# Attention scores as 64x64 matmuls in TensorE's four quadrants, plain buffers for the FFN's operands, and outputs nine f tiles behind the scores

## The chip, the cores and the metric

The kernel runs on one core of one Trainium2 chip. The metric is the device time of one execution in microseconds (us), and the time of a kernel is the median over its runs. Smaller is better.

## What is computed

There are 4 batches, 8 heads, 768 positions and a head dimension of 64. A banded attention feeds a two-layer FFN:

```python
k_sum = k.reshape(B, H, nb, block, D).max(axis=3)     # 24 blocks of 32 positions
v_sum = v.reshape(B, H, nb, block, D).mean(axis=3)
scores_l = scale * q @ k.T        # kept where |i - j| < 16, masked elsewhere
scores_s = scale * q @ k_sum.T + log(32)
a = softmax over [scores_l, scores_s]
x = a @ [v, v_sum]                # 3072 tokens of 512
h = max(x @ w_in, 0)              # w_in 512 x 2048
out = h * h @ w_out               # w_out 2048 x 512
```

## The kernel before, in words

**Tiles.** The 3072 positions are 24 tiles of 128, numbered g. Two tiles of x make a chunk c of 256 tokens, so there are 12 chunks. The FFN's hidden width is 16 f tiles of 128. One f tile of one chunk is called a slot. All operands are 32-bit. The FFN multiplies in a one-pass form with each operand split in a high and a low part (`xh`, `xl`, `gh`, `gl`, and two halves of `w_sb`). The attention multiplies plain 32-bit floats, and every such matmul in the code is two instructions in the trace.

**A slot.** `ffn1` (L318) issues 12 matmuls of 256 columns from `xh` and `xl` into a bank `ph`. `follow` then issues the 6 matmuls of 512 columns of `ffn2` (L359) for the slot two earlier (`BEHIND = 2`), with `gh` and `gl` as the stationary operand. Meanwhile ScalarE and VectorE take relu and square of `ph` (L327, L334, L339, L343).

**Attention of one tile, spread over the slots.** `steps` gives the pieces of tile g to ten steps, one step to a slot. Step 0 is `scores` (L222), steps 1 to 3 are mask, maximum and exponentials (`softmax`, L234 on VectorE, L242 on ScalarE), steps 3 and 4 the normalisation (L257), steps 5 to 7 the transposes (L270), step 8 is `outputs` (L283), step 9 is `split_x` (L301, L304), which makes `xh` and `xl`. What stands in `side` is issued in the middle of a slot, what stands in `last` at its end. A new tile begins every eight slots, so step 8 of tile g and step 0 of tile g+1 fall in the same slot, outputs first. The main loop handles tiles 6 to 23 and chunks 2 to 11.

**Scores before.** A tile's 128 queries are two groups s of 64, each with a window of 96 keys and 24 block sums, so 120 columns (`NK`). The contraction is 64 deep. `q_sb` is kept block-diagonal: partitions 0 to 63 hold group 0 in columns 0 to 63, partitions 64 to 127 hold group 1 in columns 64 to 127, and the rest is zero, set once by `memset` on GpSimd (L103). One 128x128 matmul per head then gives both groups, 8 per tile, into two buffers `s_ps` of four heads each. Loading q takes two DMAs per tile (L112). `place_k` (L157) copies the block maxima into `k_sb` with four VectorE copies.

**Outputs.** `outputs` issues 16 matmuls per tile with 64 stationary columns. Even heads write PSUM partitions 0 to 63, odd heads 64 to 127, so they use the two column halves of the array in turn.

**The start.** Tiles 0 to 5, the scores of tile 6, the preparation of the weights and the first 32 slots are issued in an order written out by hand, the string `START`: `S4.1` is `scores(4, 1)`, `TT` and `E` are the softmax of one head, `F1` and `F2` are `ffn1` and `ffn2`.

**The extra 32 bytes.** `shifted` makes the buffers of `xh`, `xl`, `gh` and `gl` 8 floats longer than needed (`SHIFT = 8`). The two or three buffers of each so begin at different addresses modulo 128 bytes: 64 and 96 for `xh`, 0 and 32 for `xl`, 64, 96 and 0 for `gh`, 32, 64 and 96 for `gl`. The weights `w_sb` all begin at 0 modulo 128.

Of the kernel before, what the change touches and what calls it, by code (L numbers as in the profile page):

```python
# [11 lines left out]
F32 = mybir.dt.float32  # L12
F32R = mybir.dt.float32r
# [16 lines left out]
NF = DF // P  # L30
NC4 = DM // P
SPARE = 1
SHIFT = 8
BEHIND = 2
NK = 96 + NB
MASKED = -1.0e9
# [20 lines left out]
F2.13 RE15v L:w13 SQ14 MU14 SQ15 MU15 F1.16 LO12a GL14v GL15v NR4.1 TT4.1 N4.1p S5.1 RE16a TT4.2 E4.1 TT4.3 MU16  # L57
F1.17 SQ16 TT4.0 E4.3 GL16v E4.2 SH12 S5.0 E4.0 RE17v AD12 F1.18 MU17 L:k7 NR4.0 L:v5 L:w15 F2.14 RE18a N4.0v
L:w14 HI13 MU18 F1.19 LO13v SQ17 CA12a GL17v SH13 F2.15 RE19a SU12v F1.20 SQ18 AD13 EV1.1v EV1.0a MU19 F2.16
GL18v RE20v CA11v F1.21 SQ19 MU20 GL19v HI15 SU11v F2.17 RE21a LO15v CA13a F1.22 MU21 SH15 SQ20 F2.18 RE22a  # L60
SU13p GL20v HI14 MU22 F1.23 SQ21 LO14a GL21v AD15 F2.19 RE23v MU23 F1.24 SQ22 SH14 CA15a GL22v AD14 F2.20 RE24v
MU24 T4.0 SQ23 F2.21 SU15p TT5.2 GL23v E5.2 TT5.1 TT5.3 T4.1 E5.1 TT5.0 F2.22 SQ24 TT5.4 TT5.5 TC4.1a GL24v
CA14a TT5.6 S6.0 TT5.7 TC4.0v E5.5 F2.23 SU14v E5.6 E5.7 S6.1 E5.0 E5.4 F1.25 E5.3 NR5.1 N5.1v F2.24 RE25v NR5.0
SQ25 MU25 F1.26 N5.0v GL25v T5.1 RE26a F1.27 SQ26 TC5.1v MU26 GL26v F2.25 RE27a SQ27 MU27 GL27v F1.28 F2.26
RE28v MU28 SQ28 GL28v F1.29 EV2.1v EV2.0v O4 RE29a SQ29 MU29 GL29v F1.30 XH4a XL4v F2.27 RE30a MU30 F1.31 SQ30
GL30v F2.28 RE31v MU31 T5.0 SQ31 F2.29 TC5.0v GL31v O5 XH5a L:v7 L:q7 XL5v L:v6
"""


# [1 line left out]
def attn_ffn_kernel(ctx: ExitStack, tc: tile.TileContext, q, k, kt, v, vt, v0, w, masks, ident, mean, out):  # L71
# [27 lines left out]
    vsum = const.tile([P, NPAIR, 32], F32, name="vsum")  # L99

    nc.vector.memset(vsum, 0.0)
    for t_ in q_sb + [e_sb] + pT:
        nc.gpsimd.memset(t_, 0.0)  # L103

    def copy(eng, out, in_):
# [15 lines left out]
    def load_v(g):  # L121
        nc.sync.dma_start(out=v_sb[g % 2][0:96], in_=v[g // NT, g % NT])
# [28 lines left out]
        nc.vector.tensor_scalar_mul(vsum[:, p, 0:NB], vsum[:, p, 0:NB], 1.0 / BLOCK)  # L151

    def place_k(g):
        dst = k_sb[g % 2].rearrange("a k (p two) j -> a k p two j", two=2)
        for par in range(2):
            for s in range(2):
                nc.vector.tensor_copy(  # L157
                    out=dst[s * 64 : s * 64 + 64, 4, :, par, :], in_=ksum[par * 64 : par * 64 + 64]
                )
# [55 lines left out]
    xh, xl = {}, {}  # L215
    s_ps, nmx, sm = {}, {}, {}

    def scores(g, half):
        s_ps[half] = ps_s.tile([P, 4, P], F32, name="s_ps")
        for i in range(4):  # L220
            h = half * 4 + i
            nc.tensor.matmul(  # L222
                s_ps[half][:, i, 0:NK], lhsT=q_sb[g % 2][:, h, :], rhs=k_sb[g % 2][:, :, h, :], start=True, stop=True
            )

    def mask_max(g, h):

        t = g % NT
        m = mask_sb[:, 0 if t == 0 else 2 if t == NT - 1 else 1, :]
        half, i = divmod(h, 4)  # L230
        if half not in nmx:
            nmx[half] = work.tile([P, 4], F32, name="nmx", tag="nmx", bufs=3)
            sm[half] = work.tile([P, 4], F32, name="sm", tag="sm", bufs=3)
        nc.vector.tensor_tensor_reduce(  # L234
            out=e_sb[:, h, 0:NK], in0=s_ps[half][:, i, 0:NK], in1=m, scale=-scale, scalar=3.0e38,
            op0=ALU.add, op1=ALU.min, accum_out=nmx[half][:, i : i + 1],
        )

# [48 lines left out]
                    start=True, stop=True,  # L287
                )

    def shifted(n, name, bufs):  # L290

        return work.tile([P, n + SHIFT], F32R, name=name, tag=name, bufs=bufs)[:, 0:n]

    def x_part(x, name, g):
        c, o = divmod(g, TPC)
        if c not in x:
            x[c] = shifted(NPAIR * CT, name, 2).rearrange("p (a b) -> p a b", b=CT)
        return x[c][:, :, o * P : (o + 1) * P]

    def high_x(g):  # L300
# [29 lines left out]
        return r  # L330

    def high_square(r):
        gh = shifted(CT, "gh", 3)
        nc.scalar.activation(gh, r, AF.Square)  # L334
        return gh

# [2 lines left out]
        nc.vector.tensor_mul(out=ph, in0=ph, in1=r)  # L339

    def low_square(ph, gh):
        gl = shifted(CT, "gl", 3)
        nc.vector.tensor_sub(out=gl, in0=ph, in1=gh.bitcast(F32))  # L343
        return gl

# [57 lines left out]
    def steps(g):  # L403


        b, t = divmod(g, NT)
        side, last = [[] for _ in range(10)], [[] for _ in range(10)]
# [3 lines left out]
        last[0] += [lambda: scores(g, 0), lambda: scores(g, 1)]  # L411
        if g + 2 < n_g:
            last[0].append(lambda: load_qk(g + 2))
        side[1].append(lambda: softmax(g, 0, 2))
        side[2].append(lambda: softmax(g, 2, 5))
        side[3] += [lambda: inverse(0), lambda: norm(0, nc.gpsimd), lambda: softmax(g, 5, 8)]
        side[4] += [lambda: inverse(1), lambda: norm(1, nc.gpsimd)]
        for n in range(3):
            side[5 + n].append(lambda n=n: turn(g, 4 * n, 4 * n + 4))
        last[8].append(lambda: outputs(g))  # L420
        if g + 2 < n_g:
            last[8].append(lambda: load_v(g + 2))
# [38 lines left out]
    def begin(op, i, j, eng):  # L461
# [14 lines left out]
            sum_v(1, i)  # L476

        elif op == "S":
            scores(i, j)
        elif op == "TT":  # L480
            mask_max(i, j)
        elif op == "E":
# [37 lines left out]
    with tc.manual_schedule(engines=None):  # L520
        for token in START.split():
            what, i, j, eng = re.fullmatch(r"(L:[a-z]+|F[12]|[A-Z]+)\.?(\d*)\.?(\d*)([avp]?)", token).groups()
            i, j = int(i or 0), int(j or 0)
            if what.startswith("L:"):
                load(what[2:], i)
            else:
                begin(what, i, j, engines.get(eng))
        tiles = {g: steps(g) for g in range(6, n_g)}

        def at(side, last, g, step):  # L530

# [85 lines left out]
```

## Time and profile before

| | |
|---|---|
| median of 3 runs | 664.42 us (664.35 to 664.96) |
| the profiled execution: its own time | 663.47 us |
| the profiled execution: span from first to last instruction | 661.7 us |
| mean granted TensorE clock | 0.992 |
| TensorE busy | 633.0 us, 4668 matmul instructions |
| VectorE, ScalarE, GpSimd busy | 404.9, 301.1, 110.6 us |
| bytes moved by DMA | 61.87 MB |

The profile is one execution, so its durations are held against its own 663.47 us, 0.95 us below the median. A row of the grouped lines reads: line, engine, operation, output<-inputs, shape, count | busy us, mean ns of one | idle time before, and what ended it. A row of the timeline reads: start, duration, engine, line, operation, and how many instructions in a row were merged. Matmuls are pipelined, and the ends of the recorded ones overlap the next ones' starts, so what a stretch of matmuls costs is read from starts alone.

### The profile page before, as it was taken

How to read it: one execution, taken by the hardware profiler on the slowest of the kernel's cores; microseconds unless marked ns; L12 is line 12 of the kernel's file. 1: busy time of each engine (PE TensorE's matmuls, PEld its weight loads, DVE VectorE, ACT ScalarE, POOL GpSimd, SP SyncE). 2: the span in 40 equal slices, each digit the busy share in tenths (PEclk: the TensorE clock that was granted, in tenths of full speed). 3: DMA queues.
4: the chain of work that ended last, by engine and by line, in shares of the span. 5: the costliest groups of instructions: out<-in, count | busy, mean ns of one | idle time of the engine just before them, and what ended most of it. 6: DMA issues, size and time to landing. Idle time of an engine off the chain costs nothing.

```text
span 661.7 us, 12338 instructions
## 1 busy us (share of the span) xinstructions
PE 633.0 (96%) x4668; PEld 566.5 (86%) x4668; DVE 404.9 (61%) x1247; ACT 301.1 (46%) x854; POOL 110.6 (17%) x87
## 2 busy tenths in 40 slices
PE   1788999999999999999999999999999999999997
PEld 1477999888889889999899998899898899988996
DVE  4678787656664684874863675865765645645332
ACT  2778867524424435335344344343444443443322
POOL 5464573401011011010010010010010110110000
PEclk9879999999999999999999999999999999999999
DMA  9999525005203314303103133212022020000000
GB/s 326 367 363 376 151 73 209 1 33 136 64 1 97 103 57 144 112 1 97 42 24 97 28 133 112 97 49 64 32 65 64 33 64 25 33 2 1 33 1 32
DMA packets 42314, 61.87 MB, mean 94 GB/s; under 512 B 27792, under 2 KB 27920, under 8 KB 40208
## 3 DMA queue, kind: packets, MB, share of 16 engines
q1 hardware_dynamic: 42256, 61.10, 28.3%
q8 instruction: 36, 0.59, 0.4%
q14 instruction: 22, 0.18, 0.1%
HBM read 54.80 MB, written 6.29 MB: 92 GB/s over the span
## 4 chain that ended last, share of the span: by engine, by line
PE 92%; DVE 3%; DMA 2%; ACT 1%; issue 1%; POOL 1%; SPq 0%; DVEq 0%; POOLq 0%; ACTq 0%
PE ph L318 41%; PE o_ps L359 39%; PE s_ps L222 7%; PE x_ps L283 3%; PE ph L263 1%; PE o_ps L129 1%; DMA kv<-in_kt 1%; DMA q_sb<-in_q 1%; DVE pT L270 1%; ACT e_sb L242 1%; DVE k_sb L157 0%; POOL e_sb L257 0%; DVE ksum L143 0%; POOL q_sb L103 0%; DVE ph L339 0%
## 5 line engine op out<-in xcount | busy, mean ns | idle before, releaser
L318 PE MATMUL ph<-xh,w_sb 128*128 128x256 f32 x1536 | 285.3, 284 | 0.7 <-ACT xh L301 0.7
L318 PEld LDWEIGHTS ph<-xh,w_sb 128*128 128x128 f32 x1536 | 248.3, 190 | 15.8 <-ACT xh L301 0.8
L359 PE MATMUL o_ps<-w_sb,gh 128*128 128x512 f32 x768 | 241.4, 395 | 0.0
L318 PE MATMUL ph<-xl,w_sb 128*128 128x256 f32 x768 | 217.0, 283 | 0.2 <-DVE xl L304 0.2
L339 DVE TENSOR_TENSOR ph<-ph,r 128x256 f32<-128x256 f32 x192 | 82.6, 431 | 157.1 <-ACT r L327 153.8
L327 ACT ACTIVATE r<-ph 128x256 f32<-128x256 f32 x179 | 68.2, 381 | 204.9 <-PE ph L318 203.7
L359 PE MATMUL o_ps<-w_sb,gl 128*128 128x512 f32 x384 | 151.3, 394 | 0.0
L318 PEld LDWEIGHTS ph<-xl,w_sb 128*128 128x128 f32 x768 | 145.5, 189 | 0.5 <-DVE xl L304 0.4
L359 PEld LDWEIGHTS o_ps<-w_sb,gh 128*128 128x128 f32 x768 | 131.1, 188 | 17.1
L257 POOL TENSOR_TENSOR e_sb<-e_sb,sm 128x480 f32<-128x480 f32 x42 | 41.7, 994 | 421.6 <-DVE nmx L234 360.9
L242 ACT ACTIVATE e_sb<-e_sb,nmx 128x120 f32<-128x120 f32 x192 | 73.9, 387 | 57.4 <-DVE nmx L234 57.4
L343 DVE TENSOR_TENSOR gl<-ph,gh 128x256 fp32r<-128x256 f32 x192 | 81.3, 424 | 29.7 <-ACT gh L334 7.1
L270 DVE STREAM_TRANSPOSE pT<-e_sb 32x256 f32<-32x256 f32 x216 | 94.2, 436 | 5.4 <-POOL e_sb L257 2.1
L334 ACT ACTIVATE gh<-r 128x256 fp32r<-128x256 f32 x192 | 80.4, 418 | 20.3 <-DVE r L329 7.7
L359 PEld LDWEIGHTS o_ps<-w_sb,gl 128*128 128x128 f32 x384 | 72.0, 188 | 17.1
L222 PE MATMUL s_ps<-k_sb,q_sb 128*128 128x120 f32 x384 | 51.4, 286 | 14.9 <-DVE k_sb L157 14.7
L222 PEld LDWEIGHTS s_ps<-k_sb,q_sb 128*128 128x128 f32 x384 | 46.9, 197 | 17.0 <-POOL w_sb L212 14.5
L234 DVE CUSTOM_DVE_ANT_0 e_sb<-s_ps,mask_sb 128x120 f32<-128x120 f32 x192 | 43.8, 274 | 5.3 <-PE ph L263 3.1
L205 POOL TENSOR_TENSOR w_raw<-w_raw 128x1024 int32<-128x1024 int32 x16 | 32.0, 2005 | 37.4 <-DVE w_raw L201 17.3
L242 ACT ACTIVATION_READ_ACCUMULATOR e_sb<-e_sb,nmx 128x1 f32 x192 | 36.1, 188 | 0.0
L283 PEld LDWEIGHTS x_ps<-pT,v_sb 128*64 128x64 f32 x768 | 24.4, 138 | 12.7 <-issue 9.5
L304 DVE TENSOR_TENSOR xl<-x_ps,xh 128x512 fp32r<-128x512 f32 x24 | 16.5, 688 | 27.0 <-ACT xh L301 27.0
(41 smaller groups left out, 293.0 us busy)
## 6 DMA issues: line engine op xcount, KB each, us to landing
w_raw<-in_w SPq DMA_DIRECT2D x16, 1024.0 KB, 10.7
k_sb<-in_k SPq DMA_DIRECT2D x24, 384.0 KB, 3.9
v_sb<-in_v SPq DMA_DIRECT2D x24, 384.0 KB, 3.7
kv<-in_kt SPq DMA_DIRECT2D x16, 384.0 KB, 5.3
q_sb<-in_q SPq DMA_DIRECT2D x48, 128.0 KB, 3.7
out<-ob SPq DMA_DIRECT2D x24, 256.0 KB, 2.0
kv<-in_vt SPq DMA_DIRECT2D x12, 384.0 KB, 4.9
vn<-in_v SPq DMA_DIRECT2D x2, 768.0 KB, 8.5
```

What stands on the lines that cost most here:

```text
L222: nc.tensor.matmul(s_ps[half][:, i, 0:NK], lhsT=q_sb[g % 2][:, h, :], rhs=k_sb[g % 2][:, :, h, :], start=True, stop=True)
L234: nc.vector.tensor_tensor_reduce(out=e_sb[:, h, 0:NK], in0=s_ps[half][:, i, 0:NK], in1=m, scale=-scale, scalar=3.0e38, op0=ALU.add, op1=AL ...
L242: nc.scalar.activation(e, e, AF.Exp, bias=nmx[half][:, i : i + 1], scale=-1.0, accum_out=sm[half][:, i : i + 1])
L257: eng.tensor_mul(out=e, in0=e, in1=sm[half].unsqueeze(2).to_broadcast([P, 4, NK]))
L270: nc.vector.transpose(out=pT[g % 2][j * 32 : j * 32 + 32, :, i * 32 : i * 32 + 32], in_=e_sb[i * 32 : i * 32 + 32, :, j * 32 : j * 32 + 32],)
L283: nc.tensor.matmul(xp[o : o + 64, h // 2, s * 64 : s * 64 + 64], lhsT=v_sb[g % 2][:, s, h * 64 : h * 64 + 64], rhs=pT[g % 2][:, h, s * 64 ...
L318: nc.tensor.matmul(ph, lhsT=w_sb[f][:, w, cc * P : (cc + 1) * P], rhs=x[c][:, cc, :], start=(n == 0), stop=(n == 3 * NC4 - 1))
L327: nc.scalar.activation(r, ph, AF.Relu)
L334: nc.scalar.activation(gh, r, AF.Square)
L339: nc.vector.tensor_mul(out=ph, in0=ph, in1=r)
L343: nc.vector.tensor_sub(out=gl, in0=ph, in1=gh.bitcast(F32))
L359: nc.tensor.matmul(o_ps[c][tt], lhsT=g_[:, ts_], rhs=w_sb[f][:, w, DM:], start=(first and n == 0), stop=(last and n == 2),)
```

## The change

Scores become 16 matmuls per tile with a contraction of 64 rows and 64 stationary columns: head parity r picks the row half of the array and the PSUM bank, query group s picks the column half. q is stored without zeros and comes in one DMA; k is stored by parity, and its block maxima are placed with one copy. One buffer `s_ps` of two banks takes the place of two of one bank. The FFN's operands lose the extra 32 bytes: each of their buffers now begins at 64 modulo 128, `w_sb` still at 0. The steps become eleven: outputs are step 9, `split_x` is step 10, and the loop starts every tile one slot earlier, so that outputs stay in their slot, scores and softmax come a slot before where they were, and scores and outputs no longer share a slot. In `START` the scores of tile 5 are both issued after the last mask of tile 4.

```diff
-SHIFT = 8
...
-F1.17 SQ16 TT4.0 E4.3 GL16v E4.2 SH12 S5.0 E4.0 RE17v AD12 F1.18 MU17 L:k7 NR4.0 L:v5 L:w15 F2.14 RE18a N4.0v
+F1.17 SQ16 TT4.0 S5.1 E4.3 GL16v E4.2 SH12 S5.0 E4.0 RE17v AD12 F1.18 MU17 L:k7 NR4.0 L:v5 L:w15 F2.14 RE18a
...
-    ps_s = ctx.enter_context(tc.tile_pool(name="ps_s", bufs=2, space=bass.MemoryType.PSUM))
+    ps_s = ctx.enter_context(tc.tile_pool(name="ps_s", bufs=1, space=bass.MemoryType.PSUM))
...
-    k_sb = [const.tile([P, 5, H, NB], F32, name=f"k_sb{i}") for i in range(2)]
+    k_sb = [const.tile([P, 5, 2, NPAIR, NB], F32, name=f"k_sb{i}") for i in range(2)]
-    q_sb = [const.tile([P, H, P], F32, name=f"q_sb{i}") for i in range(2)]
+    q_sb = [const.tile([P, 2, NPAIR, 64], F32, name=f"q_sb{i}") for i in range(2)]
...
-    for t_ in q_sb + [e_sb] + pT:
+    for t_ in [e_sb] + pT:
         nc.gpsimd.memset(t_, 0.0)
...
-        for s in range(2):
-            ps = slice(s * 64, s * 64 + 64)
-            nc.sync.dma_start(out=q_sb[g % 2][ps, :, ps], in_=q[g // NT, g % NT, ps])
+        nc.sync.dma_start(out=q_sb[g % 2], in_=q[g // NT, g % NT])
...
-        dst = k_sb[g % 2].rearrange("a k (p two) j -> a k p two j", two=2)
-        for par in range(2):
-            for s in range(2):
-                nc.vector.tensor_copy(
-                    out=dst[s * 64 : s * 64 + 64, 4, :, par, :], in_=ksum[par * 64 : par * 64 + 64]
-                )
+        nc.vector.tensor_copy(out=k_sb[g % 2][:, 4], in_=ksum.unsqueeze(1).to_broadcast([P, 2, NPAIR, NB]))
...
-    def scores(g, half):
-        s_ps[half] = ps_s.tile([P, 4, P], F32, name="s_ps")
-        for i in range(4):
-            h = half * 4 + i
-            nc.tensor.matmul(
-                s_ps[half][:, i, 0:NK], lhsT=q_sb[g % 2][:, h, :], rhs=k_sb[g % 2][:, :, h, :], start=True, stop=True
-            )
+    def scores(g, p0, p1):
+        if g not in s_ps:
+            s_ps[g] = ps_s.tile([P, 2, NPAIR, P], F32, name="s_ps")
+        for p in range(p0, p1):
+            for r, s in ((0, 0), (1, 1), (0, 1), (1, 0)):
+                rs, ss = slice(r * 64, r * 64 + 64), slice(s * 64, s * 64 + 64)
+                nc.tensor.matmul(
+                    s_ps[g][ss, r, p, 0:NK], lhsT=q_sb[g % 2][rs, s, p, :], rhs=k_sb[g % 2][rs, :, s, p, :],
+                    start=True, stop=True,
+                )
...
-            x[c] = shifted(NPAIR * CT, name, 2).rearrange("p (a b) -> p a b", b=CT)
+            x[c] = work.tile([P, NPAIR, CT], F32R, name=name, tag=name)
...
-        gh = shifted(CT, "gh", 3)
+        gh = work.tile([P, CT], F32R, name="gh", tag="gh", bufs=3)
...
-        gl = shifted(CT, "gl", 3)
+        gl = work.tile([P, CT], F32R, name="gl", tag="gl", bufs=3)
...
-        last[8].append(lambda: outputs(g))
+        last[9].append(lambda: outputs(g))
...
-        side[9].append(lambda: split_x(g))
+        side[10].append(lambda: split_x(g))
...
-        softmax(6, 0, 2)
+        softmax(6, 0, 5)
...
-                at(side, last, 2 * c + 2, f + 2)
-                at(side, last, 2 * c + 3, f - 6)
-                at(side, last, 2 * c + 4, f - 14)
+                at(side, last, 2 * c + 2, f + 3)
+                at(side, last, 2 * c + 3, f - 5)
+                at(side, last, 2 * c + 4, f - 13)
```

The order of TensorE's instructions in the main loop, around the outputs of an odd tile (`v_sb_82`) and the scores of the next, even one (`k_sb_79`), each row with its line, operation and tiles, and with how many in a row are alike. Before:

```order
L359 MATMUL o_ps<-w_sb,gh 128x512 x2
L359 MATMUL o_ps<-w_sb,gl 128x512
L283 MATMUL x_ps<-pT_87,v_sb_82 64x64 x16
L222 MATMUL s_ps<-k_sb_79,q_sb_83 128x120 x8
L318 MATMUL ph<-xh,w_sb 128x256 x2
L318 MATMUL ph<-xl,w_sb 128x256
```

After the change the scores stand alone at the end of a slot (the lines are those of the new code: L218 scores, L280 outputs, L311 `ffn1`, L352 `ffn2`):

```order
L352 MATMUL o_ps<-w_sb,gh 128x512 x2
L352 MATMUL o_ps<-w_sb,gl 128x512
L218 MATMUL s_ps<-k_sb_79,q_sb_83 64x120 x16
L311 MATMUL ph<-xh,w_sb 128x256 x2
L311 MATMUL ph<-xl,w_sb 128x256
```

One slot, that is 12 rows, further on stand the outputs of the tile before:

```order
L352 MATMUL o_ps<-w_sb,gh 128x512 x2
L352 MATMUL o_ps<-w_sb,gl 128x512
L280 MATMUL x_ps<-pT_87,v_sb_82 64x64 x16
L311 MATMUL ph<-xh,w_sb 128x256 x2
L311 MATMUL ph<-xl,w_sb 128x256
```

The scores, now 16 matmuls of 64 stationary columns, moved one slot ahead of the outputs, and both now have FFN matmuls on either side.

The second place is the beginning of VectorE's list, where the block maxima of batch 0 (`ksum`) are placed for tiles 0 and 1 and the masks of tile 0 follow. Before:

```order
L143 TENSOR_REDUCE ksum<-kv 128x24 x4
L157 COPY k_sb_79<-ksum 64x4x24 x4
L157 COPY k_sb_80<-ksum 64x4x24 x4
L234 ISA e_sb,nmx<-s_ps,mask_sb 128x120
L234 ISA nmx 128x1
```

After the change:

```order
L140 TENSOR_REDUCE ksum<-kv 128x24 x4
L151 COPY k_sb_79<-ksum 128x192
L151 COPY k_sb_80<-ksum 128x192
L231 ISA e_sb,nmx<-s_ps,mask_sb 128x120
L231 ISA nmx 128x1
```

Eight copies have become two, and nothing else moved in these rows.

More of the change, by code (lines that the diff above doesn't have):

```diff
@@ L234, in mask_max @@
         nc.vector.tensor_tensor_reduce(
-            out=e_sb[:, h, 0:NK], in0=s_ps[half][:, i, 0:NK], in1=m, scale=-scale, scalar=3.0e38,
+            out=e_sb[:, h, 0:NK], in0=s_ps[g][:, h % 2, h // 2, 0:NK], in1=m, scale=-scale, scalar=3.0e38,
             op0=ALU.add, op1=ALU.min, accum_out=nmx[half][:, i : i + 1],
@@ L288, in outputs @@
                 )
-    def shifted(n, name, bufs):
-        return work.tile([P, n + SHIFT], F32R, name=name, tag=name, bufs=bufs)[:, 0:n]
     def x_part(x, name, g):
@@ L406, in steps @@
         b, t = divmod(g, NT)
-        side, last = [[] for _ in range(10)], [[] for _ in range(10)]
+        side, last = [[] for _ in range(11)], [[] for _ in range(11)]
         if b and t < 2:
@@ L410, in steps @@
             side[6].append(lambda: place_v(g))
-        last[0] += [lambda: scores(g, 0), lambda: scores(g, 1)]
+        last[0].append(lambda: scores(g, 0, NPAIR))
         if g + 2 < n_g:
@@ L419, in steps @@
             side[5 + n].append(lambda n=n: turn(g, 4 * n, 4 * n + 4))
-        last[8].append(lambda: outputs(g))
+        last[9].append(lambda: outputs(g))
         if g + 2 < n_g:
-            last[8].append(lambda: load_v(g + 2))
-        side[9].append(lambda: split_x(g))
+            last[9].append(lambda: load_v(g + 2))
+        side[10].append(lambda: split_x(g))
         if b and t in (3, 4) and b + 1 < B:
@@ L478, in begin @@
         elif op == "S":
-            scores(i, j)
+            scores(i, 2 * j, 2 * j + 2)
         elif op == "TT":
@@ L530, in at @@
         def at(side, last, g, step):
-            if g in tiles and 0 <= step < 10:
+            if g in tiles and 0 <= step < 11:
                 side += tiles[g][0][step]
@@ L571, in _layouts @@
 def _layouts(q, k, v):
-    qt = q.reshape(B, H, NT, 2, 64, D)
-    qd = np.zeros((B, NT, 2, D, H, 64), q.dtype)
+    qd = q.reshape(B, NPAIR, 2, NT, 2, 64, D).transpose(0, 3, 2, 6, 4, 1, 5)
     kp = np.zeros((B, H, S + 2 * WINDOW, D), k.dtype)
```

27 lines of the change are left out of this document (13 added, 14 removed).

## The prediction

> **What bounds the kernel now.** I read the page first, then the busy time by stretches, the groups by shape, and TensorE's timeline around one tile. The page's busy line and its chain of work:
>
> ```profile
> PE 633.0 (96%) x4668; PEld 566.5 (86%) x4668; DVE 404.9 (61%) x1247; ACT 301.1 (46%) x854; POOL 110.6 (17%) x87
> ...
> PE 92%; DVE 3%; DMA 2%; ACT 1%; issue 1%; POOL 1%; SPq 0%; DVEq 0%; POOLq 0%; ACTq 0%
> PE ph L318 41%; PE o_ps L359 39%; PE s_ps L222 7%; PE x_ps L283 3%; PE ph L263 1%; PE o_ps L129 1%; DMA kv<-in_kt 1%; DMA q_sb<-in_q 1%; DVE pT L270 1%; ACT e_sb L242 1%; DVE k_sb L157 0%; POOL e_sb L257 0%; DVE ksum L143 0%; POOL q_sb L103 0%; DVE ph L339 0%
> ```
>
> By stretches (length, then busy time of PE, PEld, DVE, ACT, POOL, granted clock, DMA share, GB/s):
>
> ```profile
> 0.00:16.50 16.50, 1.96 (x9) 1.99 (x10) 7.76 (x14) 4.58 (x4) 9.00 (x11) 1.00 0.94 326
> ...
> 49.50:66.00 16.50, 13.99 (x137) 12.13 (x136) 13.34 (x24) 13.91 (x31) 8.10 (x5) 1.00 1.03 376
> 66.00:149.00 83.00, 83.00 (x601) 75.64 (x601) 58.87 (x146) 50.23 (x102) 34.24 (x16) 1.00 0.29 94
> 149.00:151.00 2.00, 1.09 (x15) 0.75 (x11) 1.04 (x6) 0.70 (x2) 0.00 (x0) 1.00 0.35 55
> 151.00:640.00 489.00, 488.82 (x3632) 441.07 (x3632) 296.75 (x958) 199.96 (x633) 40.91 (x45) 1.00 0.20 61
> ```
>
> From 66 us to 640 us TensorE is never idle but for 1 us (149 to 151), at the full clock. There every TensorE nanosecond is a nanosecond of the kernel, and VectorE (61% in the last row) and ScalarE (41%) have room. Before 66 us TensorE waits and DMA is full. So the change is priced by what it does to TensorE's stream, tile by tile, and separately at the start.
>
> **What scores and outputs cost now.** TensorE around one tile, from the timeline:
>
> ```profile
> 304.59 0.40 PE L318 MATMUL ph<-xh,w_sb 128*128 128x256 f32 x2
> ...
> 318.66 0.40 PE L318 MATMUL ph<-xh,w_sb 128*128 128x256 f32 x2
> ...
> 321.48 0.40 PE L318 MATMUL ph<-xh,w_sb 128*128 128x256 f32 x2
> ...
> 324.07 0.39 PE L359 MATMUL o_ps<-w_sb,gl 128*128 128x512 f32 x1
> 324.39 1.15 PE L283 MATMUL x_ps<-pT,v_sb 128*64 128x64 f32 x32
> 325.47 2.04 PE L222 MATMUL s_ps<-k_sb,q_sb 128*128 128x120 f32 x16
> 327.28 0.48 PE L318 MATMUL ph<-xh,w_sb 128*128 128x256 f32 x2
> ...
> 330.18 0.40 PE L318 MATMUL ph<-xh,w_sb 128*128 128x256 f32 x2
> ```
>
> A plain slot takes 321.48 - 318.66 = 2.82 us. The two slots from 321.48 to 330.18 take 8.70, so outputs and scores together cost 8.70 - 2 x 2.82 = 3.06 us. The scores' 16 instructions take 327.28 - 325.47 = 1.81, or 113 ns each: 0.94 ns per column of 120.
>
> The outputs alone between FFN matmuls stand at one place of the start:
>
> ```profile
> 137.88 0.40 PE L318 MATMUL ph<-xh,w_sb 128*128 128x256 f32 x2
> ...
> 139.19 0.28 PE L318 MATMUL ph<-xl,w_sb 128*128 128x256 f32 x1
> 139.40 1.15 PE L283 MATMUL x_ps<-pT,v_sb 128*64 128x64 f32 x32
> 140.48 0.50 PE L318 MATMUL ph<-xh,w_sb 128*128 128x256 f32 x2
> ...
> 142.02 0.63 PE L359 MATMUL o_ps<-w_sb,gh 128*128 128x512 f32 x2
> ...
> 143.41 0.40 PE L318 MATMUL ph<-xh,w_sb 128*128 128x256 f32 x2
> ```
>
> `ffn1` and `ffn2` from 140.48 to 143.41 take 2.93, 0.11 more than a plain slot; the last `ffn1` matmul ahead takes 0.21 instead of 0.12; the outputs themselves 1.08. A section of half-array matmuls on its own so costs 1.08 + 0.09 + 0.11 = 1.28 us. Their 32 instructions of 64 columns run two at a time: one after the other they would take 32 x 64 x 0.94 ns = 1.93 us, more than the whole section, and two at a time 0.96. What is left, 1.28 - 0.96 = 0.32 us, is the price of going into such a section and out of it.
>
> **The change in the main loop, step by step.** Tiles 7 to 23, 17 in all, have their scores there.
>
> *Scores.* 16 matmuls are 32 instructions of 120 columns. With four quadrants working at once they take 32 x 113 / 4 = 0.90 us, and with 0.32 for the section 1.22. The lower bound is the same with nothing for the section, 0.90. For the upper one I take two at a time, as the outputs run: 1.81 + 0.32 = 2.13. No row shows four at a time; I take 1.22, because the outputs' halves do overlap fully and one output pass (1.08 / 32 = 34 ns) shows instructions following each other nearly as fast as 28 ns asks.
>
> *Outputs.* They now pay their own way in and out: 1.28.
>
> *Sum.* 1.22 + 1.28 = 2.50 against 3.06: 0.56 us less per tile, 17 x 0.56 = 9.5 us. A rule speaks against this split. The Trainium skill, "TensorEngine Tiling (Array Packing)", Key Properties, says that a change of tiling mode (not just of tile) drains the TensorE. The rows agree, and put 0.32 us on a pair of such changes; keeping scores and outputs in one slot would still need three changes where the new order has four.
>
> *The 32 bytes.* Slots are 16.89 / 6 = 2.815 us long from 304.59 to 321.48, and these six go through all three `gh` and `gl` addresses twice. The chunk before, which has the other `xh` and `xl` buffers:
>
> ```profile
> 281.80 0.40 PE L318 MATMUL ph<-xh,w_sb 128*128 128x256 f32 x2
> ...
> 295.89 0.40 PE L318 MATMUL ph<-xh,w_sb 128*128 128x256 f32 x2
> ```
>
> Five slots take 14.09, 2.818 each. Between the two sets of addresses lie 0.003 us a slot, over 192 slots 0.6 us. The new addresses (64 modulo 128) are among the old ones of `xh`, `gh` and `gl`. I take nothing, and 2 us either way for the range, three times that difference.
>
> *Softmax one slot earlier.* It meets `split_x` with three heads instead of two in a slot. ScalarE's rows:
>
> ```profile
> L242 ACT ACTIVATE e_sb<-e_sb,nmx 128x120 f32<-128x120 f32 x192 | 73.9, 387 | 57.4 <-DVE nmx L234 57.4
> L334 ACT ACTIVATE gh<-r 128x256 fp32r<-128x256 f32 x192 | 80.4, 418 | 20.3 <-DVE r L329 7.7 <-PE o_ps L359 7.3
> L327 ACT ACTIVATE r<-ph 128x256 f32<-128x256 f32 x179 | 68.2, 381 | 204.9 <-PE ph L318 203.7 <-DVE gl L343 1.1
> L242 ACT ACTIVATION_READ_ACCUMULATOR e_sb<-e_sb,nmx 128x1 f32 x192 | 36.1, 188 | 0.0
> ...
> L301 ACT CAST xh<-x_ps 128x512 fp32r<-128x512 f32 x24 | 14.1, 586 | 34.5 <-PE x_ps L283 34.4
> ```
>
> 3 x (0.387 + 0.188) + 0.586 + 0.381 + 0.418 = 3.11 us in a slot of 2.82: 0.3 late. `gh` is used two slots later, 5.6 us, so this stays hidden, and the next slot gives it back. If that cover were gone, 0.3 us twice a chunk, in 10 chunks, would be 6 us. The scores' new waits are on the one `s_ps`, whose last reader is the softmax five slots ahead, and on TensorE's own scores eight slots ahead: nothing. SyncE's loads of q and k behind the scores come a slot earlier and v's as before; they are for two tiles on.
>
> **The start.** Tiles 4 to 6 have their scores in the full stretch from 66 us. Half a tile of scores:
>
> ```profile
> 86.06 0.28 PE L318 MATMUL ph<-xl,w_sb 128*128 128x256 f32 x1
> 86.17 1.04 PE L222 MATMUL s_ps<-k_sb,q_sb 128*128 128x120 f32 x8
> 86.98 0.72 PE L359 MATMUL o_ps<-w_sb,gh 128*128 128x512 f32 x2
> ...
> 88.47 0.40 PE L318 MATMUL ph<-xh,w_sb 128*128 128x256 f32 x2
> ```
>
> It costs 0.81, and 88.47 - 86.98 = 1.49 is 0.09 more than half a slot: 0.90. New: 0.45 + 0.32 = 0.77. Four such halves (tiles 4 and 6) save 0.13 each, 0.5; tile 5, now in one piece, 1.80 - 1.22 = 0.6. Together 1.1 us.
>
> Ahead of 66 us, VectorE places the maxima, TensorE computes tile 0's scores (the chain's piece), and ScalarE follows:
>
> ```profile
> 12.48 3.31 DVE L157 COPY k_sb<-ksum 64x96 f32<-64x96 f32 x8
> 14.54 3.67 PE s_ps L222 x16
> 16.72 0.28 DVE L234 CUSTOM_DVE_ANT_0 e_sb<-s_ps,mask_sb 128x120 f32<-128x120 f32 x1 [0.94 <-issue]
> 17.73 0.18 ACT L242 ACTIVATION_READ_ACCUMULATOR e_sb<-e_sb,nmx 128x1 f32 x1
> 17.82 1.13 ACT L197 ACTIVATE w_raw<-w_raw 128x1024 int32<-128x1024 uint32 x1
> ```
>
> Eight copies become two, and 3.67 us of scores about half. But DMA is full (share 0.94 to 1.03) and ScalarE's next work is on weights that it brings, so at most the 1.8 us of half the scores is gained and perhaps nothing, or a little is lost where waits fall anew. I take 1.0, about the middle. One q DMA of long rows for two of short ones, and two fewer memsets on GpSimd, lie in the same second.
>
> **Sum.** 9.5 + 1.1 + 1.0 = 11.6 us off the profiled 663.47 gives 651.9; its median stands 0.95 higher, so 664.42 - 11.6 = **652.8 us**.
>
> **Rivals.**
>
> *A. Only two instructions run at a time (slower).* The two passes of one matmul need the same quadrant and stand next to each other in the program. If TensorE starts instructions only in order, the second pass holds up the next matmul, and no more than two passes ever overlap. Then scores cost 2.13 and with the outputs 3.41, 0.35 more than now: 17 x 0.35 = 6.0; four halves 0.90 + 0.32 against 0.90, 1.3; tile 5 2.13 against 1.80, 0.3. With 0.5 from the copies at the start: 664.42 + 7.1 = 671.5. It decides once the 32 passes take over 3.06 - 1.28 - 0.32 = 1.46 us, that is below 2.5 at a time. For it: the outputs never show more than two, having two halves only. Against it: with strict order the first pass of the outputs would start alone, yet within their first 60 ns two are recorded:
>
> ```profile
> 324.38:324.45 0.07, 0.06 (x2) 0.06 (x4) 1.00 0.00 0
> ```
>
> By that strict order this rival would be the forecast: the Trainium skill, "TensorE: Matmul & The Clock Gate", What overlaps and what doesn't, has matmuls in program order in start and end without reordering. The window above speaks against it for passes of one matmul. Chance 0.15.
>
> *B. Three at a time on average, or weight loads that limit.* 1.21 + 0.32 + 1.28 = 2.81, 0.25 less per tile: 4.3, halves and tile 5 0.3, start 0.8: 659.0. Nothing in the trace speaks for three rather than four. Chance 0.07.
>
> *C. Something outside the scores gives back half:* the late slots on ScalarE (6 us) or the addresses (1% of 192 slots, 5.4 us). 652.8 + 5.5 = 658.3. Against it: the rows above. Chance 0.06.
>
> **How the numbers follow.** Forecast 0.72, A 0.15, B 0.07, C 0.06. Within the forecast the section price may vary by 0.1 us a tile (1.7), the start by 1, the addresses by 2: added in squares 2.8, so 650.0 to 655.6. The range reaches to B and C: 649.5 to 659.5; A is left out. Over 0.2% (1.3 us, about what a measurement of this kernel can tell from no change) faster: 0.72 + 0.07 + 0.06 less 0.02 for a C that gives everything back, 0.83. The same: those 0.02. Slower: A's 0.15.
>
> **What would show it.** In the profile after, scores count 768 instructions, about 28 ns apart, and a section of about 1.22 us with FFN matmuls on both sides; outputs 1.28; a plain slot still 2.81 to 2.82; TensorE without idle time from about 66 us. Scores 55 ns apart or more are A. Slots of other length are the addresses, idle time of TensorE ahead of L352 or L311 is ScalarE. I am wrong if the main loop shrinks by other than 17 times the tile's difference.

## The result and the profile after

The changed kernel takes 644.92 us (median of 4 runs, 644.11 to 646.57) against 664.58 us before (664.35 to 664.96; a fourth run of it was made beside the kernel after): a ratio of 0.9707, 95% interval 0.9687 to 0.9727. That is 19.7 us faster where 11.6 had been forecast, outside the range. The profiled execution after took 646.57 us, 1.65 above the median, with a span of 644.8.

The page's busy line and chain of the kernel after:

```profile
PE 609.8 (95%) x5052; PEld 536.3 (83%) x5052; DVE 403.3 (63%) x1223; ACT 300.4 (47%) x854; POOL 108.8 (17%) x85
...
PE ph L311 42%; PE o_ps L352 40%; PE x_ps L280 4%; PE s_ps L218 4%; PE ph L260 1%; DMA k_sb<-in_k 1%; PE o_ps L126 1%; DMA w_raw<-in_w 1%; DVE pT L267 1%; DVE ksum L140 1%; ACT e_sb L239 0%; DVE k_sb L151 0%; ACT w_raw L189 0%; POOL e_sb L2
```

TensorE still is the path nearly everywhere. The scores fell from 7% of the chain to 4%, though they are 768 instructions now instead of 384. Two stretches of the kernel after (length, busy time of PE, PEld, DVE, ACT, POOL, clock, DMA share, GB/s):

```profile
49.50:66.00 16.50, 13.90 (x126) 11.93 (x125) 12.96 (x23) 12.90 (x27) 8.09 (x5) 0.91 1.02 409
...
151.00:640.00 489.00, 486.03 (x4004) 432.60 (x4003) 300.88 (x951) 204.12 (x644) 40.86 (x45) 1.00 0.19 61
```

In the long stretch TensorE is now idle for 3 us; before it was not idle at all. TensorE around tile 13, from the timeline after:

```profile
309.83 0.40 PE L311 MATMUL ph<-xh,w_sb 128*128 128x256 f32 x2
...
312.59 0.40 PE L311 MATMUL ph<-xh,w_sb 128*128 128x256 f32 x2
...
316.71 1.05 PE L218 MATMUL s_ps<-k_sb,q_sb 64*64 64x120 f32 x32 [1.20 <-issue]
317.69 0.50 PE L311 MATMUL ph<-xh,w_sb 128*128 128x256 f32 x2
...
320.63 1.15 PE L280 MATMUL x_ps<-pT,v_sb 128*64 128x64 f32 x32
321.71 0.50 PE L311 MATMUL ph<-xh,w_sb 128*128 128x256 f32 x2
...
324.57 0.40 PE L311 MATMUL ph<-xh,w_sb 128*128 128x256 f32 x2
...
327.33 0.40 PE L311 MATMUL ph<-xh,w_sb 128*128 128x256 f32 x2
```

Three things are to be seen. A plain slot is 312.59 - 309.83 = 2.76 us long, and so is 324.57 to 327.33; before it was 2.82. This difference of 0.055 us, times 192 slots, is 10.6 us that nobody had counted. The 32 instructions of scores take 317.69 - 316.71 = 0.98 us instead of 1.81. And TensorE stands idle for 1.20 us ahead of these scores. What VectorE does then:

```profile
313.62 1.80 DVE L267 STREAM_TRANSPOSE pT<-e_sb 32x256 f32<-32x256 f32 x4
315.45 0.43 DVE L332 TENSOR_TENSOR ph<-ph,r 128x256 f32<-128x256 f32 x1
316.02 0.42 DVE L336 TENSOR_TENSOR gl<-ph,gh 128x256 fp32r<-128x256 f32 x1
316.36 0.25 DVE L151 COPY k_sb<-ksum 128x192 f32<-128x192 f32 x1
```

The copy of the block maxima (`place_k`, L151) ends at 316.36 + 0.25 = 316.61, and the scores start 0.10 later. At tile 7 the trace names it as what TensorE waited for:

```profile
168.24 1.05 PE L218 MATMUL s_ps<-k_sb,q_sb 64*64 64x120 f32 x32 [0.93 <-DVE k_sb L151]
```

From start to start, the step from the last `ffn2` matmul to the scores takes 1.31, 1.60 and 1.24 us at tiles 7, 13 and 19 instead of 0.33: 3.2 us in all. These tiles are the second of their batch, whose copy VectorE reaches after the transposes of the first.

### The profile page after: what moved, and what is told of

Same layout as the page of the kernel before. It is cut to its first block, busy times and chain, and to the rows that moved or that the text cites. A ratio compares the mean times of both kernels' runs of the same rounds, so it can differ in the third digit from the quotient of the medians.

```text
span 644.8 us, 13041 instructions
## 1 busy us (share of the span) xinstructions
PE 609.8 (95%) x5052; PEld 536.3 (83%) x5052; DVE 403.3 (63%) x1223; ACT 300.4 (47%) x854; POOL 108.8 (17%) x85
## 2 busy tenths in 40 slices
DMA packets 20429, 61.92 MB, mean 96 GB/s; under 512 B 2832, under 2 KB 2960, under 8 KB 18320
## 4 chain that ended last, share of the span: by engine, by line
PE 92%; DVE 3%; DMA 2%; ACT 1%; issue 1%; POOL 0%; SPq 0%; DVEq 0%; POOLq 0%; ACTq 0%
PE ph L311 42%; PE o_ps L352 40%; PE x_ps L280 4%; PE s_ps L218 4%; PE ph L260 1%; DMA k_sb<-in_k 1%; PE o_ps L126 1%; DMA w_raw<-in_w 1%; DVE pT L267 1%; DVE ksum L140 1%; ACT e_sb L239 0%; DVE k_sb L151 0%; ACT w_raw L189 0%; POOL e_sb L254 0%; ACT w_raw L185 0%
## 5 line engine op out<-in xcount | busy, mean ns | idle before, releaser
L311 PE MATMUL ph<-xh,w_sb 128*128 128x256 f32 x1536 | 280.4, 282 | 1.5 <-DVE gl L336 0.9
L311 PEld LDWEIGHTS ph<-xh,w_sb 128*128 128x128 f32 x1536 | 243.6, 188 | 18.8 <-issue 3.0
L352 PE MATMUL o_ps<-w_sb,gh 128*128 128x512 f32 x768 | 239.6, 393 | 0.0
L311 PE MATMUL ph<-xl,w_sb 128*128 128x256 f32 x768 | 213.9, 278 | 0.2 <-DVE xl L297 0.2
L352 PE MATMUL o_ps<-w_sb,gl 128*128 128x512 f32 x384 | 151.5, 395 | 0.0
L352 PEld LDWEIGHTS o_ps<-w_sb,gh 128*128 128x128 f32 x768 | 131.0, 188 | 17.8 <-DVE ob L105 0.3
L311 PEld LDWEIGHTS ph<-xl,w_sb 128*128 128x128 f32 x768 | 144.9, 189 | 0.5 <-DVE xl L297 0.4
L352 PEld LDWEIGHTS o_ps<-w_sb,gl 128*128 128x128 f32 x384 | 72.5, 189 | 14.8
L231 DVE CUSTOM_DVE_ANT_0 e_sb<-s_ps,mask_sb 128x120 f32<-128x120 f32 x192 | 44.0, 275 | 15.9 <-PE s_ps L218 10.6
L218 PE MATMUL s_ps<-k_sb,q_sb 64*64 64x120 f32 x768 | 27.3, 281 | 21.3 <-DVE k_sb L151 15.4
L218 PEld LDWEIGHTS s_ps<-k_sb,q_sb 64*64 64x64 f32 x768 | 21.2, 140 | 29.3 <-DVE k_sb L151 15.8
L280 PEld LDWEIGHTS x_ps<-pT,v_sb 128*64 128x64 f32 x768 | 25.6, 143 | 12.8 <-issue 9.7
```

The costliest lines, as they stand in the source:

```text
L218: nc.tensor.matmul(s_ps[g][ss, r, p, 0:NK], lhsT=q_sb[g % 2][rs, s, p, :], rhs=k_sb[g % 2][rs, :, s, p, :], start=True, stop=True,)
L231: nc.vector.tensor_tensor_reduce(out=e_sb[:, h, 0:NK], in0=s_ps[g][:, h % 2, h // 2, 0:NK], in1=m, scale=-scale, scalar=3.0e38, op0=ALU.ad ...
L280: nc.tensor.matmul(xp[o : o + 64, h // 2, s * 64 : s * 64 + 64], lhsT=v_sb[g % 2][:, s, h * 64 : h * 64 + 64], rhs=pT[g % 2][:, h, s * 64 ...
L311: nc.tensor.matmul(ph, lhsT=w_sb[f][:, w, cc * P : (cc + 1) * P], rhs=x[c][:, cc, :], start=(n == 0), stop=(n == 3 * NC4 - 1))
L352: nc.tensor.matmul(o_ps[c][tt], lhsT=g_[:, ts_], rhs=w_sb[f][:, w, DM:], start=(first and n == 0), stop=(last and n == 2),)
```

## The experiments

Each run is compared with runs of the kernel before on the same chip; those had medians of 663.8 to 664.2 us. Two theories of the 0.055 us a slot stood at first: the 32 bytes, or DMA's traffic (packets under 512 bytes fell from 27792 to 2832, since q no longer comes in short rows).

**The bytes alone, and everything but the bytes.** The first run is the kernel before with one edit:

```diff
-SHIFT = 8
+SHIFT = 0
```

> The kernel before with SHIFT = 0, nothing else. Theory, the bytes: plain slots become 2.76 instead of 2.815 us long because the buffers of xh, xl, gh and gl begin at 64 modulo 128 bytes, 192 slots x 0.055 = 10.6 us: 654 us. Rival, the DMA: slots became shorter because q no longer arrives in rows of 256 bytes (packets under 512 bytes fell from 27792 to 2832): slots stay at 2.815, 664.5 us. My prediction's own term said 664.5 give or take 2.

Measured: 654.97 us, ratio 0.9865 (0.9841 to 0.9890). The second is the kernel after with `shifted` and `SHIFT = 8` back on all four operands:

> The kernel after with the 32 bytes put back on all four operands. Theory, the bytes: plain slots 2.815 again, 645 + 10.6 = 655.5 us. Rival, the DMA: slots stay at 2.76, 645 us.

Measured: 653.83 us, ratio 0.9847 (0.9832 to 0.9862). A plain slot of the first, then of the second, from their timelines:

```profile
300.63 0.40 PE L318 MATMUL ph<-xh,w_sb 128*128 128x256 f32 x2
303.39 0.40 PE L318 MATMUL ph<-xh,w_sb 128*128 128x256 f32 x2
```

```profile
300.98 0.40 PE L316 MATMUL ph<-xh,w_sb 128*128 128x256 f32 x2
303.81 0.40 PE L316 MATMUL ph<-xh,w_sb 128*128 128x256 f32 x2
```

2.76 without the bytes, 2.83 with them, whatever the scores and q's DMA are like. The bytes cost about 9 us in either kernel. DMA as the cause is refuted.

**Which operand.** The bytes back on two of the four operands of the kernel after (`shifted` in `x_part` alone, or in `high_square` and `low_square` alone):

> The kernel after with the 32 bytes put back on xh and xl alone. Theory, the bytes, if each matmul is slowed by its own operand: the 12 matmuls of ffn1 return to about 118.5 ns from 114, those of ffn2 stay at 228.5 ns: 12 x 4.5 ns = 0.05 us a slot, 645 + 9 = 654 us. Rival, the DMA: 645 us.

Measured: 653.67 us (0.9844, 0.9829 to 0.9858).

> The kernel after with the 32 bytes put back on gh and gl alone. Theory, the bytes, if each matmul is slowed by its own operand: the 6 matmuls of ffn2 return to about 232 ns from 228.5, those of ffn1 stay at 114 ns: 6 x 3.7 ns = 0.02 us a slot, 645 + 4 = 649 us. Rival, the DMA: 645 us.

Measured: 645.07 us (0.9714, 0.9695 to 0.9733). So it is `xh` and `xl`, the moving operand of `ffn1`. The 4 us that I gave to `gh` and `gl` don't show.

**Which addresses.** Four runs give the buffers of `xh` and `xl` 128 bytes more and a place in them (off is 0 or 8 or 16 floats):

```diff
-            x[c] = work.tile([P, NPAIR, CT], F32R, name=name, tag=name)
+            o_ = {"xh": 0, "xl": 16}[name]
+            x[c] = work.tile([P, NPAIR * CT + 32], F32R, name=name, tag=name)[:, o_ : o_ + NPAIR * CT].rearrange(
+                "p (a b) -> p a b", b=CT
+            )
```

> The kernel after with 128 bytes added to each buffer of xh and xl, so that all still begin at 64 modulo 128 but no longer a multiple of 1024 bytes apart. Theory, the phase modulo 128 bytes of xh and xl sets the pace: 645 us, plain slots 2.76. Rival, any offset between the buffers slows them, because they must be a multiple of 1024 bytes apart: 653.7 us, as with the 32 bytes.

Measured: 648.53 us (0.9775, 0.9747 to 0.9802): neither theory's number.

> As the run with 128 bytes added, but xl begins 64 bytes further: xh at 64 modulo 128, xl at 0. Theory, a start that is no multiple of 64 bytes costs: none here, 645 us. Rival, xh and xl of different phase cost: 653.7 us.

Measured: 653.34 us (0.9845, 0.9822 to 0.9869).

> As the run with 128 bytes added, but xh and xl both begin 32 bytes further, all four buffers at 96 modulo 128. Theory, a start that is no multiple of 64 bytes costs: every matmul of ffn1, 653.7 us or more (in the kernel before only half of the buffers began so). Rival, only buffers of different phase cost: 645 us.

Measured: 653.06 us (0.9835, 0.9810 to 0.9860).

> As the run with 128 bytes added, but xh and xl both begin 64 bytes further, all four buffers at 0 modulo 128, as the weights do. Theory, a start that is no multiple of 64 bytes costs: 645 us. Rival, the phase against the weights' costs (64 is the good one, 0 is not): slower than 645, up to 654 us.

Measured: 654.74 us (0.9869, 0.9841 to 0.9898). Multiples of 64 bytes are slow too, and buffers of one and the same phase as well: the theories of alignment by itself fall. What was left is the place relative to the weights, which begin at 0. Two runs tell this from an address of its own, by 64 bytes ahead of everything, and ahead of `xh` once more in the second:

```diff
+    nc.vector.memset(const.tile([P, 16], F32, name="pad"), 0.0)
     mask_sb = const.tile([P, 3, NK], F32, name="mask_sb")
...
+    nc.vector.memset(work.tile([P, 16], F32, name="pad2", bufs=1), 0.0)
     xh, xl = {}, {}
```

> The kernel after with 64 bytes put ahead of everything in SBUF: weights now at 64 modulo 128, xh, xl, gh and gl at 0. Theory, what counts is the distance from the weights (64 modulo 128 is the good one), since TensorE reads a moving operand and loads the next weights at the same time: 645 us. Rival, xh and xl must themselves begin at 64: slow as with both at 0 modulo 128, 654.7 us.

Measured: 644.57 us (0.9703, 0.9685 to 0.9722).

> The kernel after with 64 bytes put ahead of everything and 64 more ahead of xh: weights at 64 modulo 128, xh, xl, gh and gl at 64 as in the kernel after. Theory, the distance from the weights counts, here 0: about 654 us. Rival, the own address of xh and xl counts: 645 us.

Measured: 654.66 us (0.9858, 0.9833 to 0.9883). Four plain slots of the first of these two, and five of the second:

```profile
299.75 0.40 PE L312 MATMUL ph<-xh,w_sb 128*128 128x256 f32 x2
...
310.79 0.40 PE L312 MATMUL ph<-xh,w_sb 128*128 128x256 f32 x2
```

```profile
300.60 0.40 PE L313 MATMUL ph<-xh,w_sb 128*128 128x256 f32 x2
...
314.70 0.40 PE L313 MATMUL ph<-xh,w_sb 128*128 128x256 f32 x2
```

11.04 / 4 = 2.76 and 14.10 / 5 = 2.82. In the second run `xh`, `xl`, `gh` and `gl` keep their place modulo 128 and are slow; in the first they have changed it and are fast. Modulo 256 their own place can't be it either: the first `xh` begins at byte 191360 in the fast run here and in the slow one with both at 0, and only what lies ahead of it, the weights among it, stands 64 bytes further. `ffn1` reads nothing there but the weights, so I take the distance from them as what counts.

**How fine the distance counts.** The run with 128 bytes added was still unexplained. Three runs move `xh`, and all buffers behind it, by 128, 256 and 2048 bytes (`pad2` alone, of 32, 64 or 512 floats):

> The kernel after with 128 bytes put ahead of xh, so that xh, xl, gh and gl all lie 64 modulo 256 from the weights (192 in the kernel after). Theory, the distance counts modulo 256: the three buffers of four that were moved by 128 or 384 in the run with 128 bytes added to each lost 3.5 us, so all of them lose about 4.5: 649.5 us. Rival, it counts modulo 128, and that run lost by something else: 645 us.

Measured: 652.81 us (0.9831, 0.9816 to 0.9846), worse than the 649.5 expected. That estimate counted three of four buffers as moved in the run with 128 bytes added. By their addresses only the second `xh` and the second `xl` were at a new place modulo 256, which is every second chunk; with all four moved the loss is about twice as large (0.9707 to 0.9831 against 0.9707 to 0.9775).

> The kernel after with 256 bytes put ahead of xh, so that xh, xl, gh and gl again lie 192 modulo 256 from the weights. Theory, the distance counts modulo 256: 645 us. Rival, it counts modulo 512 or 1024, where only the distance of the kernel after is a good one: 649 us or more.

Measured: 644.25 us (0.9695, 0.9678 to 0.9712).

> The kernel after with 2048 bytes put ahead of xh, so that xh, xl, gh and gl lie 2048 bytes further from the weights. Theory, the distance counts modulo 256 bytes or less: 645 us, and the slower matmuls of a slot (117 to 121 ns instead of 113) stay the first five, which is a matter of their place in the slot. Rival, address bits as high as 2048 count: the slower matmuls become those of the last two column blocks of x, or all of them, and the time moves by over 1 us.

Measured: 643.71 us (0.9698, 0.9680 to 0.9717). The slower matmuls stay the first five: 118, 117, 117, 122 and 118 ns from one start to the next, then 113 (medians over the plain slots), as in the kernel after. Five plain slots with 128 bytes, and four with 256:

```profile
299.58 0.40 PE L312 MATMUL ph<-xh,w_sb 128*128 128x256 f32 x2
...
313.65 0.40 PE L312 MATMUL ph<-xh,w_sb 128*128 128x256 f32 x2
```

```profile
299.82 0.40 PE L312 MATMUL ph<-xh,w_sb 128*128 128x256 f32 x2
...
310.86 0.40 PE L312 MATMUL ph<-xh,w_sb 128*128 128x256 f32 x2
```

2.81 and 2.76. The runs on addresses in one table; the distance is the start of a buffer less the start of the weights, modulo 256 bytes, by the addresses in the compiled kernels (the weights' tiles are a multiple of 256 bytes apart), and the slot is the median of the 122 to 141 plain slots between 151 and 640 us:

| kernel | first `xh`, `xl` | second `xh`, `xl` | plain slot | time |
|---|---|---|---|---|
| before | 192, 0 | 224, 32 | 2.817 | 664.58 |
| after; 64 bytes ahead of everything; 256 or 2048 ahead of `xh` | 192, 192 | 192, 192 | 2.760 | 643.7 to 644.9 |
| after, bytes on `gh`, `gl` | 192, 192 | 192, 192 | 2.759 | 645.07 |
| before without the bytes | 192, 192 | 192, 192 | 2.760 | 654.97 |
| after, bytes on all four | 192, 0 | 224, 32 | 2.817 | 653.83 |
| after, bytes on `xh`, `xl` | 192, 0 | 224, 32 | 2.818 | 653.67 |
| 128 bytes added to each | 192, 192 | 64, 64 | 2.806 | 648.53 |
| the same, `xl` 64 further | 192, 0 | 64, 128 | 2.815 | 653.34 |
| the same, both 32 further | 224, 224 | 96, 96 | 2.810 | 653.06 |
| the same, both 64 further | 0, 0 | 128, 128 | 2.827 | 654.74 |
| 64 bytes ahead of everything, 64 more ahead of `xh` | 0, 0 | 0, 0 | 2.820 | 654.66 |
| 128 bytes ahead of `xh` | 64, 64 | 64, 64 | 2.813 | 652.81 |

Of the distances tried (0, 32, 64, 96, 128, 192, 224) only 192 is fast; with `xh` alone at 192 and `xl` at 0 the slots were slow (`xl` alone at 192 was not tried). The run that stood between the theories has the good distance in every second chunk. Its timeline, two slots of a chunk's first half and two of the second half:

```profile
255.84 0.40 PE L314 MATMUL ph<-xh,w_sb 128*128 128x256 f32 x2
258.65 0.40 PE L314 MATMUL ph<-xh,w_sb 128*128 128x256 f32 x2
...
280.56 0.40 PE L314 MATMUL ph<-xh,w_sb 128*128 128x256 f32 x2
283.32 0.40 PE L314 MATMUL ph<-xh,w_sb 128*128 128x256 f32 x2
```

This chunk has the good distance throughout; its slots are 2.81 long until a section of scores and outputs has passed, and 2.76 from there on. The kernel after shows the same once, at the start of its main loop:

```profile
158.73 0.40 PE L311 MATMUL ph<-xh,w_sb 128*128 128x256 f32 x2
161.54 0.40 PE L311 MATMUL ph<-xh,w_sb 128*128 128x256 f32 x2
...
178.91 0.40 PE L311 MATMUL ph<-xh,w_sb 128*128 128x256 f32 x2
181.68 0.40 PE L311 MATMUL ph<-xh,w_sb 128*128 128x256 f32 x2
```

2.81 ahead of the scores at 168.24, 2.77 behind them, with the same buffers. So the distance does not set the pace alone: with the good one TensorE's stream has a slower and a faster pace, and can change over at a section. It can change for the worse too: in the run with the old steps (below) a slot is 2.76 long ahead of its first section (160.63 to 163.39), 2.81 behind it (171.60 to 174.41), and 2.76 again behind the second. What decides between the two no run shows. With the other distances no plain slot was shorter than 2.78.

**The late copy.** The kernel after with `place_k` a step earlier:

```diff
-            side[0].append(lambda: place_k(g))
...
+        if g + 1 < n_g and (g + 1) // NT and (g + 1) % NT < 2:
+            side[7].append(lambda: place_k(g + 1))
         for n in range(3):
             side[5 + n].append(lambda n=n: turn(g, 4 * n, 4 * n + 4))
```

> The kernel after with the copy of the block maxima (place_k) issued one step earlier, ahead of the last four transposes of the tile before. Theory, three of the four stalls of TensorE (0.99, 1.27 and 0.91 us ahead of the scores of tiles 7, 13 and 19) are VectorE reaching this copy late: they go, 645 - 3.2 = 641.8 us. Rival, the stalls move to another wait of the same slots: 645 us.

Measured: 640.88 us (0.9642, 0.9616 to 0.9668). TensorE around tile 13, now without idle time:

```profile
304.07 0.40 PE L311 MATMUL ph<-xh,w_sb 128*128 128x256 f32 x2
...
306.83 0.40 PE L311 MATMUL ph<-xh,w_sb 128*128 128x256 f32 x2
...
309.69 1.05 PE L218 MATMUL s_ps<-k_sb,q_sb 64*64 64x120 f32 x32
310.67 0.51 PE L311 MATMUL ph<-xh,w_sb 128*128 128x256 f32 x2
...
314.70 0.50 PE L311 MATMUL ph<-xh,w_sb 128*128 128x256 f32 x2
...
317.56 0.40 PE L311 MATMUL ph<-xh,w_sb 128*128 128x256 f32 x2
```

The stalls are gone, and nothing took their place.

**Outputs and scores in one slot again.** The kernel after with the old steps:

```diff
-        last[9].append(lambda: outputs(g))
+        last[8].append(lambda: outputs(g))
...
-        side[10].append(lambda: split_x(g))
+        side[9].append(lambda: split_x(g))
...
-                at(side, last, 2 * c + 2, f + 3)
+                at(side, last, 2 * c + 2, f + 2)
```

(and `load_v`, the other two `at` lines and the first `softmax` likewise).

> The kernel after with the outputs back at step 8, so that a tile's outputs and the next tile's scores share a slot again, outputs first. Theory, by the rows of the kernel after: one pair of entry and exit less per tile (326 + 151 - 231 = 246 ns go, about 150 for outputs to scores come, 0.1 us x 17 = 1.6 us), and the outputs again cover the late copy of the block maxima (3.2 us): 640 us. Rival, sharing a slot delays something that the separation had hidden (softmax behind split_x, or the banks): 645 us or more.

Measured: 638.12 us (0.9604, 0.9582 to 0.9626), the rival refuted. Its timeline at tile 13:

```profile
307.35 0.40 PE L311 MATMUL ph<-xh,w_sb 128*128 128x256 f32 x2
...
310.11 0.40 PE L311 MATMUL ph<-xh,w_sb 128*128 128x256 f32 x2
...
312.96 1.15 PE L280 MATMUL x_ps<-pT,v_sb 128*64 128x64 f32 x32
314.04 1.05 PE L218 MATMUL s_ps<-k_sb,q_sb 64*64 64x120 f32 x32
315.02 0.50 PE L311 MATMUL ph<-xh,w_sb 128*128 128x256 f32 x2
...
317.87 0.40 PE L311 MATMUL ph<-xh,w_sb 128*128 128x256 f32 x2
```

Outputs and scores together now cost 317.87 - 310.11 - 2 x 2.76 = 2.24 us. Apart, in the run ahead of this, they cost 317.56 - 306.83 - 3 x 2.76 = 2.45. The last run has both edits:

> The kernel with outputs and scores in one slot again, and the copy of the block maxima one step earlier as well. Theory, where they share a slot the outputs already cover that copy but for one stall of about 0.4 us ahead of tile 7: 637.7 us. Rival, the copy ahead of the transposes delays the transposes and with them the outputs: 639 us or more.

Measured: 637.97 us (0.9607, 0.9592 to 0.9621), the same as with the one edit. Either beats both kernels of the study, the kernel after by about 7 us.

## Why the prediction was wrong

The three parts of the change, each by two runs (differences of ratios times 664 us, each uncertain by about 2 us). The first part holds all that belongs to the new layout: the matmuls in quadrants, q in one DMA, one copy for the maxima, one `s_ps`, and the new `START`.

- the quadrants, with outputs and scores in one slot: 0.9865 to 0.9604, **17.3 us** less;
- the 32 bytes: 1 to 0.9865 in the old kernel, 0.9847 to 0.9707 in the new one, **9.0 and 9.3 us** less;
- the new order of steps: 0.9604 to 0.9707, **6.8 us** more.

**The step that failed is "The 32 bytes": "I take nothing, and 2 us either way".** It is 9 us: a plain slot is 2.76 us long without the bytes and 2.817 with them, in either kernel. The mechanism, not a size, was missing. I compared the two sets of addresses that the trace of before holds and found 0.003 us between them. But both are slow sets: one has `xh` at 192 and `xl` at 0, the other 224 and 32. Their agreement says nothing of a set that the trace does not hold. I then reasoned that 64 modulo 128 was already among the old addresses; that looked at each buffer by itself, where the distance from the weights counts, modulo 256, for `xh` and `xl` together. Three times the difference of two cases that happened to agree was no bound for a third. Rival C had the addresses give back half; it too had them on the wrong side.

**The rest of the sum held, partly because errors cancelled.** With nothing for the bytes the forecast was 652.8; the kernel after with the bytes put back took 653.83. Its main loop, from the first slot of chunk 2 to the last matmul, is 499.22 us long (149.62 to 648.84) against 507.69 before (149.98 to 657.67): 8.5 us less, where 9.5 had been forecast. A tile's section gained 3.06 - 2.45 = 0.61 instead of 0.56, which is 10.4 in 17 tiles; stalls ahead of the scores took 2.0 of it back: 2.7 us in this run (1.29, 1.38 and 1.02 from the last `ffn2` matmul to the scores of tiles 7, 13 and 19 instead of 0.33) against 0.7 before (sections of 3.54 and 3.24 at tiles 7 and 19 instead of 3.06). By terms:

- *Scores.* 1.22 forecast; in the run with the early copy the slot with scores is 310.67 - 306.83 = 3.84 long, 1.08 more than a plain one, and the slot with outputs and the one behind it 1.37. Together 2.45, forecast 2.50. Where outputs stand alone, at the end of the main loop of the kernel after, they cost 594.10 - 587.31 - 2 x 2.76 = 1.27, forecast 1.28, which leaves 1.18 for the scores. Four quadrants at once was right. Rival A is refuted: 32 instructions in 0.98 us are 3.7 at a time, if each takes the 113 ns of one with 120 columns before, and within the first 0.07 us four are recorded on PE. Rival B's 1.21 + 0.32 = 1.53 for the scores isn't seen either. The first 0.07 us:

```profile
316.71:316.78 0.07, 0.07 (x4) 0.07 (x7) 0.07 (x1) 0.00 (x0) 0.00 (x0) 1.00 0.00 0
```

  Which passes run side by side, those of one matmul or of four, these rows don't say, so the order in which TensorE starts them stays open.
- *"The scores' new waits ... nothing."* Wrong. I followed the waits on `s_ps` and on TensorE, but not the one on `place_k`, which is an old wait. Before, 1.08 us of outputs stood between the last `ffn2` matmul and the scores and hid most of it. At tile 7 the trace of before shows what was left, with 1.33 us from outputs to scores instead of 1.08:

```profile
170.38 1.15 PE L283 MATMUL x_ps<-pT,v_sb 128*64 128x64 f32 x32
171.71 2.28 PE L222 MATMUL s_ps<-k_sb,q_sb 128*128 128x120 f32 x16 [0.18 <-DVE k_sb L157]
```

  Moving the scores to a slot of their own took that cover away: 3.2 us in three tiles. With 17 x (2.45 - 2.24) = 3.6 us for the second section per tile this makes 6.8. About 0.5 us of stall is left in the run with the old steps too (its first two sections cost 2.69 and 2.31 instead of 2.24), so the profiles account for 6.3, where the times of the runs differ by 6.8, give or take 2.
- *"Keeping scores and outputs in one slot would still need three changes where the new order has four."* I wrote this and did not price it: the new order costs 0.21 us a tile.
- *The start from 66 us on*, 1.1 forecast: from the `ffn1` row at 66.44 to the main loop it is 83.54 us before, and with the bytes put back 82.35 (67.27 to 149.62), 1.2 less.
- *The start ahead of 66 us*, 1.0 forecast: not seen. That row stands at 66.44 before, at 66.70 after and at 67.27 with the bytes put back. One profile can't settle it: in four executions with one and the same `START` (the kernel after and the three runs on the order of steps) the main loop begins between 145.27 and 149.72, and the one after had a granted clock of 0.91 in the stretch from 49.5 us, where before had 1.00.
- *ScalarE's late slots*: hidden, as forecast. Behind the last tile, where no softmax runs any more, the slots are 2.76 like those beside it, and the waits of PE hold no time for `gh`.

**What stays open** is why the distance counts. TensorE reads a moving operand and loads the next weights at the same time (in the kernel after, matmuls are recorded for 95% of the span and weight loads for 83%), so that the two meet in SBUF is at hand, but no run separates it from other causes. The Trainium skill, "TensorE: Matmul & The Clock Gate", Step-by-step: what each phase is for, says that loading the next weights takes no SBUF read bandwidth from the running matmul. Here 64 bytes more between the weights and the operands behind them cost 10 us (644.57 to 654.66); whether by a loss of read bandwidth no run shows.

## What to carry to other kernels

A part of a change that looks like bookkeeping, such as a buffer's start, gets a run of its own, or a range that reaches beyond what the old trace happens to contain: two equal cases in a trace bound only themselves. When a step moves, ask what had hidden its waits at the old place, the waits that don't change above all. And a change that wins can hold a part that loses: here undoing the new order of steps was worth another 7 us.

## What the runs showed of the hardware that was not expected

- The pace of `ffn1`'s 32-bit one-pass matmuls depends on where the moving operand lies against the stationary one: 113 ns from one to the next for seven of the twelve in a slot at a distance of 192 bytes modulo 256, mostly 117 to 122 at the others. Moving `gh` and `gl`, the stationary operand of `ffn2`, cost nothing that shows (645.07 against 644.92 us).
- With the good distance, slots of 2.81 and of 2.76 us were seen on the same buffers; the changes seen in the main loop fell on a section of other matmuls or on a change of chunk.
- Ten times fewer short DMA packets change nothing in TensorE's pace (2.817 us a slot before, with 27792 packets under 512 bytes, and 2.817 in the kernel after with the bytes, with 2832).
- In four quadrants, 32-bit matmuls of 64x64 ran about 3.7 at a time (32 instructions of 120 columns in 0.98 us; at 128x128 one took 113 ns).
